# U of batches 2 to 7 as seven block products, with sums of x taken from the P V banks

## The chip, the cores and the metric

The kernel runs on one core of one Trainium2 chip. The metric is the device time of one launch in microseconds (us), lower is better: 511.04 us before the change, the median of 3 runs (510.77 to 511.21). TensorE (PE) multiplies, loads its stationary operand by LDWEIGHTS (PEld) and writes PSUM; VectorE (DVE) and ScalarE (ACT) read PSUM and SBUF; GpSimd (POOL) works on SBUF; every DMA is issued from SyncE's queue (SP), in order.

## The reference

```python
# attention: 8 batches, 8 heads, S = 576, head size 64
scores = scale * np.matmul(q, k.transpose(0, 1, 3, 2))
# heads 0-3: the last 32 positions; heads 4-7: earlier positions of the same residue mod 32
attn = softmax(np.where(masks, scores, -1e9))
x = np.matmul(attn, v)                      # as (B, S, 512)
# feed-forward with a spatial gate, d_ff = 1024
h = np.maximum(x @ w_in, 0.0)
u, v = h[..., :512], h[..., 512:]
v_n = (v - mean(v)) / np.sqrt(var(v) + 1e-6)
v_s = np.einsum('ts,bsd->btd', w_spatial, v_n) + b_spatial[None, :, None]
out = (u * v_s) @ w_out
```

## The kernel before

**Numbers.** A float32 value is kept as a rounded fp32r part and an fp32r remainder, and a product is three matmuls (high x high, high x low, low x high: `PROD`, L69). Splitting a value takes two instructions: `rnd` (L383, on ACT, DVE or POOL) makes the high part, `rest` (L397, on DVE or POOL) subtracts it.

**Attention** runs in 32 units, four per batch: two with local heads (`local_attention`, L471) and two with strided heads (`strided_attention`, L611), two heads each. A unit loads q, k and v, multiplies scores, makes a softmax on DVE and ACT, turns P by a DVE transpose, moves its blocks (`ptl`, `pts`) and multiplies P V into two PSUM banks `po`, from which `evac_x` (L424) writes x: ACT makes the high part, DVE the remainder. q, k, v, `kbd` (the strided k), `pp` and `pl` (P before it is turned) have two buffers each.

**Feed-forward**, per batch: `project_v` (L981, the V stage, 48 matmuls of 512 columns, then relu and normalisation in `chain`, L907), `project_u` (L997, the U stage), `gate` (L1084: the spatial product, then u times it) and `project_out` (L1130, the O stage). U is x @ w_in's left half: 8 tiles (2 halves of the sequence times 4 blocks of 128 features), each 4 x 3 matmuls of 128x288, 96 in all, and ACT writes each tile with relu (L1032). O is written as seven products of 2x2 blocks in place of eight, in a form with 7 multiplications (L1220 to L1258): sums of its operand are made on DVE or POOL (`total`), split into one of two slots `gs[0]`, `gs[1]`, multiplied into PSUM banks that go on accumulating, and combined by `keep` (a copy) and `join` (a DVE addition). All stages share four PSUM banks `m`; `held` keeps two of them out of the round for a time.

**The order** is made by a planner in the kernel (`Program.order`, L185): each operation has a due time (`key`), a cost per engine that may do it, and its dependencies; a list schedule gives each engine's sequence, which is what runs. Numbers in `KEYS` (L40) shift due times. PE runs in that order, so that it waits wherever the next matmul's operand, buffer or bank isn't ready. Batches overlap in pairs: the order of stages is V(b), O(b-1), U(b), gate(b), with one tail product for two batches, V's last 64 rows of both, after the first one's U (`moe_tail`, L1051; it needs x of both).

Of the kernel before, what the change touches and what calls it, by code (L numbers as in the profile page):

```python
# [9 lines left out]
F32 = mybir.dt.float32  # L10
# [30 lines left out]
    "a": (-4467.57, -3072.23, -4097.95, -922.09, -62.58, 1948.86, -54.07, 1313.94,),  # L41
    "v": (-1905.33, 2566.85, -1420.01, -351.81,),
    "u": (2077.2, 2507.69, 3441.61, -704.54,),
    "s": (1600.35, 689.49, 1605.62, -2112.6,),
    "t": (-863.37,),
    "o": (2205.96, 3994.67,),
    "cst": (-3153.23,),
    "wv": (1302.43, 874.44, 1384.1, 1780.19,),
    "wu": (-954.94, -624.77, 1601.45, 150.66,),
    "lead": (10.96,),  # L50
    "fill": (634.17, 3536.74, 3759.85, 2050.78, 1027.03, 2069.52,),
    "dp": (1410.82, -7913.25, 17481.82, 35293.8,),
    "dpt": (1128.82,),
    "lv": (-2407.03, -1707.29, -454.82, -254.06,),
    "lu": (1673.71, 2694.32, 1173.88, 457.25,),
    "lo": (1682.63, -1711.68, 1604.3, -4779.41,),
    "ls": (-1419.42, 1216.18, -2053.61, -239.17, 1173.72,),
    "pre": (2.84, 55.65,),
    "near": (3261.26,),
    "la": (-2830.09, -2292.21, -5019.65, -1683.98, -4639.4, -3037.2, 298.54, 1600.86,),  # L60
    "lb": (-1002.76, 2105.75, -428.93, 3194.59, 1811.71, 608.19, -588.14, 3548.95,),
# [9 lines left out]
U_FIRST = (0,)  # L71
WHOLE = ()
# [59 lines left out]

class Ring:
# [14 lines left out]
class Program:  # L148
# [3 lines left out]
    def __init__(self):  # L152
        self.ops, self.writer, self.readers, self.spare = [], {}, {}, {}
        self.tiled, self.port, self.kind = {}, {}, {}

# [176 lines left out]
def attention_moe(ctx, tc, qT, kT, ks, vl, vs, cst, eye, w_in, w_out, wsp, wtail, out):  # L332
# [11 lines left out]
    cst_sb = sb.tile([P, 3, 2 * STRIDE], F32, name="cst_sb")  # L344
    mask_l0, mask_l, mask_s = cst_sb[:, 0], cst_sb[:, 1], cst_sb[:, 2, :RA]
# [27 lines left out]
    r_bn = Ring(sb, "bn", [P, 12], F32, 3)  # L373
# [7 lines left out]
    held = set()  # L381
# [40 lines left out]
    xs = {}  # L422

    def evac_x(due, whole, x_t, o_ps, w, c0, src, dst, extra=0):  # L424
        if whole:
            evac(due - 1, w, lambda: f32(dst(0)), src, [(o_ps,)], [(x_t, 0, c0)], extra=extra)
            return
# [43 lines left out]
    def local_attention(t, due, q, kl, v, vin, kin):  # L471
        p_sb, st, x_t = p_local[t % 2], st_local[t % 2], xs[t]
# [44 lines left out]
        for u in range(nu):  # L517
# [16 lines left out]
            if not masked:  # L534
                add(
                    due - 12.5, [(DVE, 75 + 1.04 * 2 * STRIDE)], f_m,
                    [(s_ps[u % 2],), ("cst",), ("local0", t % 2)], [(p_sb, u), (st, u)],
                )

            def f_e(eng, f0=f0, u=u, m=m):  # L540
# [9 lines left out]
                [(st, u), *([(s_ps[u % 2],), ("local0", t % 2)] if masked else [])],  # L550
# [3 lines left out]
        if t in APART:  # L554
# [5 lines left out]
                [*pin, ("local0", t % 2)], [(st, u) for u in range(nu)],  # L560
# [13 lines left out]
        for i, n, slot, c0, z in LOCAL_MOVES:  # L574
            for k in range(2):
# [12 lines left out]
                ptok.append(("ptl", i, k, c0))  # L588
        for c0 in (0, 3):
            o_ps = r_po.new()  # L590
            w = 3 * LQ

            def f_v(eng, c0=c0, o_ps=o_ps):
# [13 lines left out]
                due, t in WHOLE, x_t, o_ps, w, c0, lambda o_ps=o_ps, w=w: o_ps()[:, :w],  # L607
                lambda i, c0=c0, w=w: x_t()[:, i, c0 * LQ : c0 * LQ + w],
            )

    def strided_attention(t, due, q, k, v, vin, kin):  # L611
        st, x_t = r_st.new(), xs[t]
        nu, w = 2 * SB, 2 * SB * RA
        pp = pps[t % 2]
        ptok = ("pp", t % 2)
# [4 lines left out]
        view = lambda: pp[:, :, :RA]  # L620
        scores = lambda: s_ps()[:, :w].rearrange("p (u k) -> p u k", k=RA)
        zeros_in = ("pp0", t % 2)
        each = lambda ap: ap[:, :, None].to_broadcast([P, nu, RA])

        def f_s(eng):
            for c in range(SB):
                for i in range(4):
# [6 lines left out]
                        kbd[:, t % 2, :, STRIDE + r : STRIDE + r + RA],  # L634
# [7 lines left out]
        if not masked:  # L642
# [40 lines left out]
            lambda eng: eng.transpose(turned(), pp[:]), [ptok], [(pc,)],  # L683
# [8 lines left out]
        half = RA * STRIDE // 2  # L692
# [613 lines left out]
    def setup_sel(eng):  # L1306
        eng.memset(sel, -0.5)
# [154 lines left out]
```

## Time and profile before

| | |
|---|---|
| median of 3 runs | 511.04 us |
| the profiled execution | 509.85 us |
| its span, first to last instruction | 507.8 us |
| PE, PEld busy | 495.6, 455.2 us |
| DVE, ACT, POOL busy | 344.7, 280.3, 111.7 us |
| mean granted TensorE clock | 0.99 |

Busy time of PE is pipelined: a 128x288 matmul is shown with some 296 ns, though in a dense run one starts every 133 ns. DVE instructions overlap in the same way at their ends. An "idle before" is put down to whatever ended it last.

### The profile page before, as it was taken

How to read it: one execution, taken by the hardware profiler on the slowest of the kernel's cores; microseconds unless marked ns; L12 is line 12 of the kernel's file. 1: busy time of each engine (PE TensorE's matmuls, PEld its weight loads, DVE VectorE, ACT ScalarE, POOL GpSimd, SP SyncE). 2: the span in 40 equal slices, each digit the busy share in tenths (PEclk: the TensorE clock that was granted, in tenths of full speed). 3: DMA queues.
4: the chain of work that ended last, by engine and by line, in shares of the span. 5: the costliest groups of instructions: out<-in, count | busy, mean ns of one | idle time of the engine just before them, and what ended most of it. 6: DMA issues, size and time to landing. Idle time of an engine off the chain costs nothing.

```text
span 507.8 us, 15733 instructions
## 1 busy us (share of the span) xinstructions
PE 495.6 (98%) x6398; PEld 455.2 (90%) x6398; DVE 344.7 (68%) x1069; ACT 280.3 (55%) x871; POOL 111.7 (22%) x229
## 2 busy tenths in 40 slices
PE   7599999999999999999999999999999999999997
PEld 4478898889988999899998999989998899989997
DVE  3988898988678628784488925687288841666055
ACT  5897777577546556373654765355554642235214
POOL 3553426133232013020221211121022200120000
PEclk9699999999999999999999999999999999999999
DMA  8996443422423412204224243024131020002002
GB/s 288 397 359 222 125 139 108 137 93 64 144 92 119 127 50 91 90 25 151 81 92 138 76 132 89 4 90 139 60 99 45 1 94 0 1 2 93 1 1 94
DMA packets 26247, 52.71 MB, mean 104 GB/s; under 512 B 3136, under 2 KB 11584, under 8 KB 26176
## 3 DMA queue, kind: packets, MB, share of 16 engines
q1 hardware_dynamic: 26176, 51.72, 31.0%
q8 instruction: 50, 0.82, 0.7%
q14 instruction: 21, 0.17, 0.1%
HBM read 42.27 MB, written 9.44 MB: 102 GB/s over the span
## 4 chain that ended last, share of the span: by engine, by line
PE 95%; DMA 4%; SPq 0%; issue 0%; ACT 0%
PE m L961 21%; PE m L1018 20%; PE m L1099 20%; PE m L1149 18%; PE po L700 3%; PE po L596 3%; DMA q<-qT 3%; PE s L486 2%; PE s L629 2%; PE m L1111 2%; PE m L1112 2%; DMA kbd<-ks 1%; PE po L1378 0%; SPq L420 0%; PE m L629 0%
## 5 line engine op out<-in xcount | busy, mean ns | idle before, releaser
L1099 PE MATMUL m<-wsp_sb,vn 128*128 128x288 f32 x768 | 112.9, 296 | 0.0
L1099 PEld LDWEIGHTS m<-wsp_sb,vn 128*128 128x128 f32 x768 | 105.5, 189 | 0.9
L1018 PE MATMUL m<-x,w_in_sb 128*128 128x288 f32 x768 | 105.3, 297 | 0.0
L1018 PEld LDWEIGHTS m<-x,w_in_sb 128*128 128x128 f32 x768 | 103.0, 188 | 0.6
L961 PE MATMUL m<-w_in_sb,x 128*128 128x512 f32 (+1 forms) x408 | 99.4, 398 | 0.0
L1149 PE MATMUL m<-g,w_out 128*128 128x288 f32 x672 | 92.9, 296 | 0.0
L1149 PEld LDWEIGHTS m<-g,w_out 128*128 128x128 f32 x672 | 89.9, 188 | 1.3
L961 PEld LDWEIGHTS m<-w_in_sb,x 128*128 128x128 f32 (+1 forms) x408 | 74.1, 185 | 18.3
L393 POOL TENSOR_SCALAR ptl<-pc 32x64 f32<-32x64 f32 (+3 forms) x98 | 38.5, 393 | 105.5 <-DVE pc L567 69.5
L916 DVE BATCH_NORM_STATS2 bn<-vv 128x6 f32<-128x512 f32 (+1 forms) x37 | 25.2, 683 | 47.4 <-ACT vv L911 47.1
L391 ACT CAST g<-u 128x288 fp32r<-128x288 f32 x91 | 39.0, 435 | 29.4 <-DVE u L812 13.1
L543 ACT ACTIVATE pl<-pl,ml 128x64 f32<-128x64 f32 (+1 forms) x140 | 47.0, 337 | 7.9 <-DVE ml L523 7.8
L929 POOL TENSOR_TENSOR bn<-bn,sel 128x1 f32<-128x1 f32 (+1 forms) x37 | 21.5, 582 | 130.0 <-DVE bn L924 125.2
L401 DVE TENSOR_TENSOR g<-u,g 128x288 fp32r<-128x288 f32 x98 | 43.6, 459 | 7.5 <-ACT g L391 5.2
L911 ACT ACTIVATE vv<-m 128x512 f32<-128x512 f32 (+1 forms) x37 | 21.9, 596 | 47.0 <-PE m L961 46.7
L1032 ACT ACTIVATE u<-m 128x288 f32<-128x288 f32 x56 | 22.9, 409 | 41.2 <-PE m L1018 40.5
L1121 DVE TENSOR_TENSOR u<-m,u 128x288 f32<-128x288 f32 x56 | 24.9, 453 | 30.5 <-PE m L1112 29.9
L391 ACT COPY ptl<-pc 32x320 f32<-32x320 f32 (+3 forms) x94 | 33.5, 356 | 13.7 <-DVE pc L567 11.9
L413 ACT CAST x<-po 128x288 fp32r<-128x288 f32 x60 | 22.1, 399 | 22.2 <-PE po L700 10.3
L401 DVE TENSOR_TENSOR x<-po,x 128x288 fp32r<-128x288 f32 x64 | 27.3, 447 | 8.4 <-ACT x L413 7.9
L523 DVE CUSTOM_DVE_ANT_0 pl<-s,cst_sb 128x64 f32<-128x64 f32 (+1 forms) x140 | 22.1, 215 | 14.5 <-PE s L486 14.5
L543 ACT ACTIVATION_READ_ACCUMULATOR pl<-pl,ml 128x1 f32 (+1 forms) x140 | 26.3, 188 | 0.0
(128 smaller groups left out, 632.8 us busy)
## 6 DMA issues: line engine op xcount, KB each, us to landing
q<-qT SPq DMA_DIRECT2D x32, 295.0 KB, 4.3
v_raw<-vs SPq DMA_DIRECT2D x15, 512.0 KB, 3.8
v_raw<-vl SPq DMA_DIRECT2D x16, 384.0 KB, 3.7
k<-kT SPq DMA_DIRECT2D x16, 304.0 KB, 4.5
kbd<-ks SPq DMA_DIRECT2D x32, 144.0 KB, 4.9
outT<-o SPq DMA_DIRECT2D x32, 144.0 KB, 1.9
outT<-u SPq DMA_DIRECT2D x28, 144.0 KB, 1.8
vn<-w_in SPq DMA_DIRECT2D x4, 512.0 KB, 7.5
```

The lines of the kernel that those rows point to most:

```text
L391: eng.copy(dst(), src())
L393: eng.tensor_scalar(dst(), src(), 1.0, 0.0, op0=ALU.mult, op1=ALU.add)
L401: eng.tensor_tensor(dst(), src(), f32(hi()), op=ALU.subtract)
L413: eng.copy(dst(), src())
L543: eng.activation(p_sb()[:m, u, :], src, AF.Exp, bias=st()[:m, u : u + 1], scale=SCALE if masked else -1.0, **total,)
L916: lambda eng: eng.bn_stats(bn()[:m, 0:6], v()[:m]), [(v,)], [(bn,)],
L961: eng.matmul(v_ps()[:m, :], x_at(kt)[:, a, :], w_in_sb[:, w, kt, HF:], start=(n == 0 and i == 0), stop=(n == NT - 1 and i == 2),)
L1018: eng.matmul(u_ps()[:, :HS], w_in_sb[:, w, kt, f * P : (f + 1) * P], xs[NHP * b + kt]()[:, a, r], start=(n == 0 and i == 0), stop=(n == NT ...
L1032: lambda eng, u=u, f=f, u_ps=u_ps: eng.activation(flat(u)[:, f * HS : (f + 1) * HS], u_ps()[:, :HS], AF.Relu),
L1099: eng.matmul(s_ps()[:, :HS], vn()[:, a, kt, fs], wsp_sb[:, w, kt, r], start=(kt == 0 and i == 0), stop=False,)
L1121: lambda eng, ug=ug, s_ps=s_ps: eng.tensor_tensor(ug(), s_ps()[:, :HS], ug(), op=ALU.mult),
L1149: eng.matmul(o_ps()[:, :HS], w_out_t[0]()[:, w, r, BLOCKS[name], j * P : (j + 1) * P], at(a), start=(first and r == 0 and i == 0), stop=(r ...
```

## The change

- For batches 2 to 7 U becomes `project_u_blocks`: the scheme of seven products that O has, so 7 x 2 x 2 x 3 = 84 matmuls of 128x288 in place of 96. Its left operands are blocks of w_in and four sums of them, which `in_weight_sums` makes once (5 DVE or POOL instructions for each of 4 sums x 2 halves, and the rounding); its right operands are blocks of x and four sums of them.
- The sums of x are made from the P V banks while they are there: `local_sums` one copy and one subtraction of 288 columns for a local unit, `strided_sums` six subtractions of 144 columns for a strided one. Then each sum is split into `gs` (2 halves x rnd and rest).
- The sums live in the second buffers of q, k and `kbd`, the sums of the weights in the second buffers of v, `pp` and `pl` and in a new tile. From unit 8 on (batch 2) attention has one buffer of each of these (`only`, `half`).
- U is written by `keep` (8 copies) and `join` (6 additions) without relu; the gating product makes the relu (one instruction in place of one).
- `sel` and `zeros` lose their tiles, the rings `mx` and `bn` go from 3 to 2, and all of `KEYS` has other values (two lines shown).

```diff
-    "wu": (-954.94, -624.77, 1601.45, 150.66,),
+    "wu": (1507.37, -2412.73, 850.89, 747.53,),
...
+    "su": (-798.11,),
...
+U_BLOCKS = tuple(range(2, B))
...
+    alone = NHP * U_BLOCKS[0] if U_BLOCKS else NHP * nb
+    half = lambda t: t % 2 if t < alone else 0
+    only = lambda t: () if t < alone else (1,)
...
-        q, k = r_q.new(), None
+        q, k = r_q.new(only(t)), None
...
-            v = place = r_v.new()
+            v = place = r_v.new(only(t))
...
+            homes = [r_q.new((0,)), r_k.new((0,)), *spare_k]
...
+    def local_sums(b, r, due, o_ps):
...
+        evac(due - 0.8, HS, at(2, r), lambda: o_ps[1]()[:, :HS], [(o_ps[1],)], toks(2, r))
+        add(
+            due - 0.7, [(DVE, 70 + 1.04 * HS)],
+            lambda eng: eng.tensor_tensor(at(0, r)(), at(2, r)(), o_ps[0]()[:, :HS], op=ALU.subtract),
...
+    def strided_sums(b, r, due, views):
...
+        for i, (n, hf, y) in enumerate(((1, 1, 0), (2, 1, 2), (3, 0, 1))):
+            for g, (o_ps, view) in enumerate(views):
...
+                add(
+                    due - 0.7 + 0.1 * i, [(DVE, 70 + 0.52 * HS)],
+                    lambda eng, n=n, y=y, hf=hf, view=view, part=part: eng.tensor_tensor(
+                        part(n), view()[:, RA // 2 * hf : RA // 2 * (hf + 1), :], part(y), op=ALU.subtract
...
+    def in_weight_sums():
+        key = KEYS["su"][0]
+        hv, late = r_v.new((0,)), [r_pp.new((0,)), r_pl.new((0,))]
...
+        for i, (name, a, b, op) in enumerate((
+            ("s1", "21", "22", ALU.add), ("s3", "11", "21", ALU.subtract),
+            ("s2", "s1", "11", ALU.subtract), ("s4", "12", "s2", ALU.subtract),
+        )):
...
+    def project_u_blocks(b, key):
...
+        product(key, "11", direct(0, 0), xb, True)
+        product(key + step, "s1", summed(0, 1), zb, True)
+        for j in range(2):
+            keep(key + step, 0, j, xb[j])
+        product(key + 2 * step, "s2", summed(1, 0), xb, False)
...
+        product(key + 3 * step, "s4", direct(1, 1), zb, False)
...
+        product(key + 4 * step, "s3", summed(2, 1), xb, False)
+        for j in range(2):
+            join(key + 4 * step, 1, j, zb[j])
+        wb = [r_pm.new(held) for _ in range(2)]
+        product(key + 5 * step, "12", direct(1, 0), wb, True)
...
+        product(key + 6 * step, "22", summed(3, 0), xb, False)
...
-                    lambda eng, ug=ug, s_ps=s_ps: eng.tensor_tensor(
-                        ug(), s_ps()[:, :HS], ug(), op=ALU.mult
+                    lambda eng, ug=ug, s_ps=s_ps: (
+                        eng.scalar_tensor_tensor(
+                            ug(), ug(), 0.0, s_ps()[:, :HS], op0=ALU.max, op1=ALU.mult
```

PE in the U stage of batch 2, before: tile after tile, each of the four blocks of x in turn (`x_13` to `x_16`).

```order
L1018 MATMUL m_68_2983<-x_13_1569,w_in_sb_62 128x288 x3
L1018 MATMUL m_68_2983<-x_14_1837,w_in_sb_62 128x288 x3
L1018 MATMUL m_68_2983<-x_15_2036,w_in_sb_62 128x288 x3
L1018 MATMUL m_68_2983<-x_16_2172,w_in_sb_62 128x288 x3
L1018 MATMUL m_69_3015<-x_13_1569,w_in_sb_62 128x288 [waits DVE_49]
```

The same stage after the change (line 1163; `g` holds a split sum of x, `pp_3` and `pl_3` a sum of weights): the products of four blocks stand among each other, and P V of unit 14 (line 721) follows, which waits for its v.

```order
L1163 MATMUL m_66_2919<-g_7_1600,pp_3_1897 128x288 [waits Activation_49,Pool_49]
L1163 MATMUL m_66_2919<-g_7_1600,pp_3_1897 128x288 x2
L1163 MATMUL m_67_2926<-g_7_1600,pp_3_1897 128x288 [waits Activation_49]
L1163 MATMUL m_67_2926<-g_7_1600,pp_3_1897 128x288 x2
L1163 MATMUL m_66_2919<-g_7_1600,pl_3_2220 128x288 [waits Pool_49]
L1163 MATMUL m_66_2919<-g_7_1600,pl_3_2220 128x288 x2
L1163 MATMUL m_67_2926<-g_7_1600,pl_3_2220 128x288 x3
L1163 MATMUL m_72_3093<-x_15_1989,w_in_sb_62 128x288 [waits DVE_49]
L1163 MATMUL m_72_3093<-x_15_1989,w_in_sb_62 128x288 x2
L721 MATMUL po_28_3098<-pts_68,v_raw_20_3055 64x2x18 [waits DMAHW0_49,PE_49]
```

So U waits for sums, their splits and bank copies on three engines; P V of units 13 and 14 now lie inside the stage and those of 15 and 16 right behind it, where before the stage began with units up to 15 done.

SP's queue around the loads of v for units 17 and 18, before; odd and even numbers of `v_raw` are the two buffers, so a load waits for the P V of the last unit but one.

```order
L420 DMA v_raw_16_2916<-vl 128x768 [waits DMAHW5_49,PE_49]
L420 DMA q_18_2988<-qT 128x590 [waits DMAHW6_49,PE_49]
L420 DMA k_10_2998<-kT 128x608 [waits DMAHW7_49]
L420 DMA v_raw_17_3193<-vs 128x1024 [waits DMAHW0_49,PE_49]
L420 DMA q_19_3200<-qT 128x590 [waits DMAHW1_49,PE_49]
L420 DMA k_11_3210<-kT 128x608 [waits DMAHW2_49]
```

The same queue after, from unit 14 of the program (`v_raw_20`) on: only even numbers, one buffer, so each load of v waits for the P V right before it.

```order
L438 DMA v_raw_20_3055<-vs 128x1024 [waits DMAHW0_49,PE_49]
L438 DMA q_28_3065<-qT 128x590 [waits DMAHW1_49,PE_49]
L438 DMA k_16_3071<-kT 128x608 [waits DMAHW2_49]
L438 DMA v_raw_22_3140<-vs 128x1024 [waits DMAHW3_49,DMAHW0_49,PE_49]
L438 DMA v_raw_24_3280<-vl 128x768 [waits DMAHW4_49,DMAHW3_49,PE_49]
L438 DMA q_30_3292<-qT 128x590 [waits DMAHW5_49,DMAHW1_49,PE_49]
```

DVE while PE is in U of batch 2 and takes P V of units 13 and 14, after the change (L419 `rest`, L791 and L806 sums of x, L1194 `join`; before, DVE held here the L401 rows on x, a softmax and nothing of U):

```order
L419 TENSOR_TENSOR g_6_1532<-kbd_67,g_6_1532 128x288 [waits Pool_49]
L457 TENSOR_SCALAR ml0_72<-ml0_72 128x10 [waits Activation_49]
L461 RECIPROCAL ml0_72<-ml0_72 128x10 [waits DVE_49]
L419 TENSOR_TENSOR x_18_3014<-po_27_2996,x_18_3014 128x288 [waits PE_49,Activation_49]
L466 TENSOR_TENSOR pl_0_74<-pl_0_74,ml0_72 128x640 [waits DVE_49]
L791 TENSOR_TENSOR q_17_2994<-kbd_67,po_26_3006 128x288 [waits Activation_49]
L419 TENSOR_TENSOR x_18_3014<-po_26_3006,x_18_3014 128x288
L1194 TENSOR_TENSOR u_5_2966<-m_68_2912,u_5_2966 128x288 [waits DMAHW5_49,DMAHW2_49,DMAHW6_49,DMAHW1_49,PE_49]
L1194 TENSOR_TENSOR u_5_2966<-m_69_2950,u_5_2966 128x288 [waits PE_49]
L1194 TENSOR_TENSOR u_5_2966<-m_66_2919,u_5_2966 128x288 [waits PE_49]
L1194 TENSOR_TENSOR u_5_2966<-m_67_2926,u_5_2966 128x288 [waits PE_49]
L806 TENSOR_TENSOR k_9_3138<-po_28_3098,q_17_2994 128x9x16 [waits Activation_49]
```

DVE gets new work in a stage in which it had little; the sums of a unit come before the bank it reads is free for the next P V.

## Rows read from the trace of the kernel before

**Rows 1.** The page: busy time by engine; the span in 40 slices for PE, DVE and the granted clock.

```profile
PE 495.6 (98%) x6398; PEld 455.2 (90%) x6398; DVE 344.7 (68%) x1069; ACT 280.3 (55%) x871; POOL 111.7 (22%) x229
PE   7599999999999999999999999999999999999997
...
DVE  3988898988678628784488925687288841666055
...
PEclk9699999999999999999999999999999999999999
```

**Rows 2.** All waits of PE: what waited for what, us in total, times, longest.

```profile
PE m L486 <- DMA q<-qT: 6.4, 1, 6.4
PE s L1378 <- DVE zeros L1332: 0.9, 1, 0.9
PE m L629 <- DMA k<-kT: 0.7, 1, 0.7
PE po L700 <- issue: 0.6, 1, 0.6
PE m L629 <- DMA q<-qT: 0.3, 1, 0.3
```

**Rows 3.** The chain that ended last, in order of time (start us, us, what): a whole U stage, a whole V stage, a whole O stage.

```profile
293.90 12.80 PE m L1018 x96
...
388.16 11.20 PE m L961 x48
...
454.63 11.10 PE m L1149 x84
```

**Rows 4.** Busy time by stretch (us; PE, PEld, DVE, ACT, POOL; granted clock; DMA share, GB/s): 60 us early, 10 us of it, a V stage with the beginning of O, and three U stages (in the first DVE makes one local unit of attention: its two remainders of x, ten maxima, the normalisation and the turn).

```profile
60.00:120.00 60.00, 60.00 (x870) 54.55 (x869) 53.50 (x192) 45.90 (x157) 21.17 (x39) 1.00 0.34 108
...
90.00:100.00 10.00, 10.00 (x56) 8.79 (x56) 9.83 (x28) 5.37 (x17) 1.53 (x3) 1.00 0.50 167
...
388.00:413.00 25.00, 25.00 (x264) 22.42 (x263) 22.12 (x59) 14.16 (x36) 5.09 (x10) 1.00 0.16 53
...
172.00:186.00 14.00, 14.00 (x198) 13.71 (x191) 4.41 (x26) 8.55 (x35) 2.23 (x7) 1.00 0.35 106
...
294.00:307.00 13.00, 13.00 (x98) 12.92 (x97) 2.06 (x4) 7.33 (x27) 2.31 (x7) 1.00 0.28 82
...
413.00:426.00 13.00, 13.00 (x98) 12.95 (x97) 0.00 (x0) 3.48 (x9) 0.00 (x0) 1.00 0.10 32
```

**Rows 5.** Groups by line and shape (busy us, mean ns of one, idle before): the additions and splits of 288 columns, an addition of 256, a remainder of 512, a scalar_tensor_tensor from PSUM, a short one, ACT's copy, relu and cast, POOL's cast.

```profile
L401 DVE TENSOR_TENSOR g<-u,g 128x288 fp32r<-128x288 f32 x98 | 43.6, 459 | 7.5 <-ACT g L391 5.2 <-POOL g L393 1.5
L1121 DVE TENSOR_TENSOR u<-m,u 128x288 f32<-128x288 f32 x56 | 24.9, 453 | 30.5 <-PE m L1112 29.9
L401 DVE TENSOR_TENSOR vn<-vv,vn 128x512 fp32r<-128x512 f32 x32 | 21.9, 686 | 3.7 <-ACT vn L391 3.6
L645 DVE SCALAR_TENSOR_TENSOR pp<-s,cst_sb 128x288 f32<-128x288 f32 x14 | 6.2, 446 | 3.0 <-PE s L629 3.0
L812 DVE TENSOR_TENSOR g<-g 128x256 f32<-128x256 f32 x6 | 2.8, 474 | 0.1
L924 DVE TENSOR_SCALAR bn<-bn 128x1 f32<-128x1 f32 x35 | 5.1, 146 | 0.4
L413 ACT COPY u<-m 128x288 f32<-128x288 f32 x28 | 11.1, 399 | 8.9 <-PE m L1149 8.8
L1032 ACT ACTIVATE u<-m 128x288 f32<-128x288 f32 x56 | 22.9, 409 | 41.2 <-PE m L1018 40.5 <-ACT u L1032 0.5
L391 ACT CAST g<-u 128x288 fp32r<-128x288 f32 x91 | 39.0, 435 | 29.4 <-DVE u L812 13.1 <-PE m L1149 8.7 <-DVE u L1121 6.4
L393 POOL TENSOR_SCALAR g<-u 128x288 fp32r<-128x288 f32 x7 | 3.0, 432 | 9.1 <-PE m L1149 6.8 <-ACT w_out L391 2.1
```

**Rows 6.** DVE in order of time (start us, us of the piece, count): a dense run of 288-column instructions; and one of 256 columns beside a POOL cast.

```profile
92.46 0.80 DVE L401 TENSOR_TENSOR g<-u,g 128x288 fp32r<-128x288 f32 x2
...
96.14 0.17 DVE L920 BATCH_NORM_AGGREGATE bn<-bn 128x2 f32<-128x6 f32 x1
...
87.08 0.42 DVE L812 TENSOR_TENSOR g<-g,g 128x256 f32<-128x256 f32 x1
87.23 1.60 POOL L393 TENSOR_SCALAR w_out<-g 128x512 fp32r<-128x512 f32 x2
87.53 0.77 DVE L812 TENSOR_TENSOR g<-g 128x256 f32<-128x256 f32 x1
```

**Rows 7.** In order of time: a P V of a strided unit with the load of v that waits for its end, and the scores of a local unit; then loads of v by their time from issue to landing (two short stretches, and the least, median and most from 120 to 480 us).

```profile
281.07 1.14 PE L700 MATMUL po<-pts,v_raw 64*64 64x36 f32 x64
282.30 0.34 SPq L420 DMA_DIRECT2D v_raw<-vl  x1
...
175.75 0.97 PE L486 MATMUL s<-k,q 64*32 64x64 f32 x72
...
v_raw<-vs SPq DMA_DIRECT2D x1, 512.0 KB, 3.8
...
v_raw<-vs SPq DMA_DIRECT2D x1, 512.0 KB, 4.3
...
DMA to landing us min/median/max: 2.9/3.7/5.2
```

**Rows 8.** PE in order of time: six records (three matmuls) of the warm-up that the planner puts into early gaps.

```profile
30.82 1.48 PE L1378 MATMUL po<-zeros 128*32 128x256 f32 x6
```

More of the change, by code (lines that the diff above doesn't have):

```diff
@@ L559, in local_attention @@
                 ),
-                [*pin, ("local0", t % 2)], [(st, u) for u in range(nu)],
+                [*pin, ("local0", half(t))], [(st, u) for u in range(nu)],
             )
@@ L733, in attention @@
         if local:
-            k = r_k.new()
+            k = r_k.new(only(t))
             load(fetch_k, k, kT[b, hp], [(k,)], P * (STRIDE + S) * 4)
@@ L746, in attention, with block_sums @@
         (local_attention if local else strided_attention)(t, due, q, k, v, [(place,)], kin)
+    def block_sums(b):
+        if b not in sums:
+            for j in range(2):
+                before = spare_k[j].users if spare_k[j] else prog.users([("k", 1, j), ("k0", 1)])
+                spare_k[j] = Place(lambda j=j: kbd[:, 1, j], before)
+            homes = [r_q.new((0,)), r_k.new((0,)), *spare_k]
+            got = lambda n: homes[n].tile() if n > 1 else homes[n]()
+            sums[b] = (
+                lambda n, r: lambda: got(n)[:, r * HS : (r + 1) * HS],
+                lambda n, r: [(homes[n], r, g) for g in range(2)],
+            )
+        return sums[b]
@@ L1036, in project_u, with product, fn, direct @@
                 )
+    in_sums = {}
+    def project_u_blocks(b, key):
+        at, tok = sums.pop(b)
+        u = [r_u.new() for _ in range(2)]
+        us[b, 0], us[b, 1] = u
+        step = 1.5
+        def product(key, name, src, bank, first):
+            w_at, w_tok = in_sums[name]
+            for r in range(2):
+                op, toks = src(r, key + 0.74 * r)
+                for j in range(2):
+                    def fn(eng, r=r, j=j, op=op):
+                        for i, (w, a) in enumerate(PROD):
+                            eng.matmul(
+                                bank[j]()[:, :HS], w_at(w, r)[:, j * P : (j + 1) * P], op(a),
+                                start=(first and r == 0 and i == 0), stop=(r == 1 and i == 2),
+                                skip_group_check=not first,
+                            )
+                    add(
+                        key + 0.74 * r + 0.37 * j, [(PE, 3 * pe_cost(P, HS))], fn,
+                        toks + w_tok[r], [(bank[j],)],
+                    )
+        def direct(k, hf):
+            return lambda r, key: (
+                lambda a: xs[NHP * b + 2 * k + r]()[:, a, hf * HS : hf * HS + HS], x_tok(NHP * b + 2 * k + r),
+            )
+        def summed(n, slot):
+            def src(r, key):
+                g = gs[slot]
+                op = lambda a: g()[:, 2 * r + a]
+                split(key - KEYS["pre"][0], HS, op, (g, r), at(n, r), tok(n, r))
+                return op, [(g, r, 0), (g, r, 1)]
+            return src
+        def keep(key, hf, f, bank):
+            evac(key, HS, block(u[hf], f), lambda: bank()[:, :HS], [(bank,)], [(u[hf], f)])
+        def join(key, hf, f, bank):
+            dst = block(u[hf], f)
+            add(
+                key, [(DVE, 70 + 1.04 * HS)],
+                lambda eng: eng.tensor_tensor(dst(), bank()[:, :HS], dst(), op=ALU.add),
+                [(bank,)], [(u[hf], f)],
+            )
+        xb, zb = ([r_pm.new(held) for _ in range(2)] for _ in range(2))
+        held.update(x.n % 4 for x in xb)
+        product(key, "11", direct(0, 0), xb, True)
+        product(key + step, "s1", summed(0, 1), zb, True)
+        for j in range(2):
+            keep(key + step, 0, j, xb[j])
+        product(key + 2 * step, "s2", summed(1, 0), xb, False)
+        for j in range(2):
+            keep(key + 2 * step, 1, 2 + j, zb[j])
+        product(key + 3 * step, "s4", direct(1, 1), zb, False)
+        for j in range(2):
+            keep(key + 3 * step, 1, j, xb[j])
+        product(key + 4 * step, "s3", summed(2, 1), xb, False)
+        for j in range(2):
+            join(key + 4 * step, 1, j, zb[j])
+        wb = [r_pm.new(held) for _ in range(2)]
+        product(key + 5 * step, "12", direct(1, 0), wb, True)
+        for j in range(2):
+            join(key + 5 * step, 1, 2 + j, xb[j])
+        product(key + 6 * step, "22", summed(3, 0), xb, False)
+        held.clear()
+        for j in range(2):
+            join(key + 6 * step, 0, j, wb[j])
+            keep(key + 7 * step, 0, 2 + j, xb[j])
@@ L1277, in attention_moe @@
     starts, knots, at = [], [(0.0, NHP)], 0.0
+    lasts = lambda kind, b: cost[kind] - 1.5 * (kind == "u" and b in U_BLOCKS)
     for kind, b in plan:
@@ L1283, in attention_moe @@
         starts.append(at)
-        at += cost[kind]
+        at += lasts(kind, b)
     if nb <= lead:
```

196 lines of the change are left out of this document (131 added, 65 removed).

## Prediction

> **What bounds the kernel now.** Read the waits of PE first [rows 2]: 8.9 us in all, every one of them on the input, the set-up or an "issue" at the start; after that PE waits for nothing. The page says the same [rows 1]: PE is at 9 tenths or more from the third slice to the last but one, and the granted clock is near full (2.4 GHz) in every slice but the second, in which PE stood waiting. So the chain that ended last is PE's own list of matmuls, and its stages give the price of one [rows 3]: U 12.80 us for 96, 133.3 ns each; V 11.20 for 48 of 512 columns, 233.3 ns; O 11.10 for 84, 132.1 ns. The 296 ns that the page shows for a matmul is its length, not its price. DVE is the next engine, 344.7 us [rows 1], but unevenly spread: 53.5 of 60 us early, 22.1 of 25 in a V stage, 2.1 and 0.0 of 13 in two U stages [rows 4]. PE did not wait in any of these, not even where DVE was busy for 9.83 of 10 us.
>
> The reader should take two questions from this: how many matmuls go, and whether anything new can come later than PE in a list that has no slack of its own.
>
> **The sum, part by part.** All against the profiled execution: 509.85 us, of which 507.8 are the span and 2.05 lie around it; the median of the runs, 511.04, is 1.19 above it, and I add that at the end.
>
> *Removed on PE.* Six batches x (96 - 84) = 72 matmuls x 133.3 ns = **-9.6 us**, all on the path, since U runs back to back on PE [rows 3]. The new products have the same shape, so the price is the same (132.1 ns by the O stage, which has this very form: -9.5). Nothing else on PE changes, except the warm-up: the order has 14 warm-up matmuls where it had 12, and one costs 1.48/3 = 0.5 us [rows 8]. They stand in early gaps where PE would wait anyway: 0 to +1.0; the order of loads at the start also changes, and q of unit 2, for which PE waited 6.4 us [rows 2], now has some 200 KB less ahead of it in SP's queue, about half a us at the early rate. I take 0 for the start, with -0.7 to +1.0 as bounds.
>
> *Added on DVE, per batch of 2 to 7.* Eight remainders (four sums x two halves), six joins and two sums of a local unit, all of 288 columns, at 43.6/98 = 0.445 us [rows 5]: 7.1 us. Twelve sums of 144 columns from PSUM: no such row stands in the trace; a one-column instruction takes 0.15 and a 288-column one 0.45, so 1.8 to 5.4 us; I take the line through 288 and 512 columns (0.459 and 0.686 us, so 1.0 ns a column), 0.31 each, 3.7. Together 10.8, in six batches 65 us. The sums of the weights add 20 additions and 8 remainders of 256 columns on DVE at 0.474 [rows 5]: 13.3, once. DVE comes to 423 us of some 500, 85%; in a dense run a 288-column instruction follows the last after (96.14 - 92.46)/10 = 0.368 us [rows 6], and by that it is nearer 80%.
> The gating product costs what it did (446 for a scalar_tensor_tensor, 453 for the product) and so does ACT's copy in place of the relu (399, 409) [rows 5]. ACT gets the local copies and most casts of the sums, about 34 x 0.42 = 14 us on 280 [rows 1], and POOL some 40 short casts, 17 us on 112: neither is near its limit.
>
> *Where the added work meets PE.* In the U stage itself DVE has 8 remainders and 6 joins, 5 to 6 us, plus the sums of the units whose P V stand there, about 4 us, in some 14 us with two units' P V and scores: it fits into what was 0 to 4.4 us of work [rows 4]. The O stage runs the same chain of split, product, keep and join, with more of it, and 84 matmuls take 11.10 us with no wait [rows 3]. So I put these chains at 0, with +0.4 us for the place where one of the pairs' tail products waits for the last unit of attention, whose sums and remainders now come one behind the other on DVE (bounds 0 and 1.5: three pairs at one 288-column instruction more, 0.45, each). If a bank is read too late, what queues behind it on PE is the next P V.
>
> *The early third.* Here the cover is thin. Before, DVE did 53.5 us in 60 [rows 4]. The sums of the weights (13.3) and batch 2's sums of x (4.5) make 71.3. The order takes three units of attention out of it (at the start of batch 2's U, P V is done up to unit 12, before up to 15), and a unit's DVE work is 4.4 us (the first U stage of [rows 4]): 58.1, in 58 us or so of PE. Dense, at 0.368 in place of 0.445, it is about 48. Between the two a wait of PE is likely but short. I take +1.2 us; bounds 0 and 5.
>
> *One buffer in place of two.* From unit 8 on a load of v can start only when the last P V is over. SP issues it 0.1 us after that (282.21, 282.30) and it lands after 2.9 to 5.2 us, median 3.7; with q right behind it 3.8 and 4.3 [rows 7]. In the order PE has this much work between two P V of a batch's neighbours: scores 0.97 [rows 7] and 24 matmuls x 0.133, 4.1 us, at the shortest for a strided unit. Twelve places have such short distances: five of 4.0 to 4.1 us, five of 4.5 to 4.8, and two of 3.7 before a local unit, with its smaller load. Against 0.1 + 3.7 + 0.1 none waits, against 4.3 + 0.2 five wait 0.4 (2 us), and if all landed like the slowest, 5.4 in all: 5 x 1.35 + 5 x 0.75 + 2 x 1.7 = 13.9 us. I take +0.5 (nearest to the median). q and k have 8 us and more between two scores, so they are not late.
> The Trainium skill ("Trainium Kernel Development and Optimization", Best Practices) says to double-buffer so that DMA overlaps compute, and this part does the opposite. The trace of before can't show the loss, since its loads had two buffers; that loss is the third rival.
>
> *POOL beside DVE.* A 256-column addition with both inputs in SBUF took 0.77 us where its neighbour took 0.42, while a POOL cast was running [rows 6]; so each added cast of 0.43 on POOL can cost DVE up to 0.35. Forty of them, all met, are 14 us of DVE, most of it where DVE is idle; it is inside the bounds of the early third and gives no term.
> The Trainium skill ("SBUF — State Buffer", Who interferes with whom) calls the port pair of DVE and GpSimd an exclusive lock, held for the whole instruction, which an addition with two SBUF inputs takes too; that row agrees with it. By that rule the sums kept in SBUF cost more than by the plain row of 0.45, at most the same 14 us of DVE.
>
> **Sum:** 509.85 - 9.6 + 0 + 0.4 + 1.2 + 0.5 = 502.35; with 1.19 for the median **503.5 us**.
>
> **The rivals.**
> 1. *DVE becomes the bound* in the early third and in batches 2 to 4. For it: 58 us of work for 58 us of PE, and DVE's waits for other engines don't vanish. Against it: PE did not wait beside 9.83 of 10. Price: the upper bound 5 early plus 0.5 in each of two later pairs, in place of 1.2: 508.3 us at most, 506 to 508.
> 2. *The saving is eaten in the U stage*: four of seven products wait for a split and banks for a keep or join. For it: split is ACT 0.435 and DVE 0.45, 0.9 us and the hand-overs, and now lies ahead of PE in a stage that only had ACT behind it. Against it: the O stage. Price: 0.4 us x 4 products x 6 batches = 9.6, so 511 to 513: no change or a little slower.
> 3. *The single buffer of v*, the other side: at each of the twelve places PE stands until v lands. It decides from the point where these waits pass 511.0 - 503.0 = 8.0 us, 0.67 a place; with 4.24 us of PE work at the mean place and 0.2 for the hand-overs that is when v lands after 4.7 us on the mean, where median and most are 3.7 and 5.2 [rows 7]; at the most, 13.9 us, the time is 503 + 13.4 = 517. For it: one load of v with q behind took 4.3. Against it: nothing else big is on the queues in these stretches (DMA share 0.10 to 0.35 in the V and U stages [rows 4]).
>
> **Chances.** The forecast, 501 to 505.5: 0.68. The first rival, 505.5 to 508.5: 0.14. The second: 0.07, about half of it within 0.2% (1 us, what a measurement of this kernel can tell from no change). The third: 0.07 slower than 512. Better than 501 (a shorter start and no wait at all): 0.04. So faster 0.87, same 0.04, slower 0.09. The range 500.8 to 508.5 leaves out the slower cases and little of the better one, some 15 in 100; the forecast's own range is 501 to 505.5.
>
> **What the profile of after would show.** Right: 84 matmuls in a U stage; PE's busy time down by 8 to 10 us; DVE near 420; PE's waits after the start adding up to 1 to 4 us, some before P V on v, some in the first 130 us on DVE. Rival 1 shows as PE waiting on DVE rows between 90 and 140 us; rival 2 as waits of line 1163 on ACT or DVE in every batch; rival 3 as waits of line 616 or 721 on v, twelve times. A start that ends PE's first wait much later than 17 us, or a granted clock below full after a wait, would make the forecast wrong altogether.

## The result, and the profile after

The changed kernel is slower: 516.35 us as the median of 4 runs (515.21 to 517.83) against 510.9 us of before beside it, a ratio of 1.0112 with a 95% interval of 1.0082 to 1.0141. I had forecast 503.5 us and a gain. The profiled execution, the slowest of the four, took 517.83 us; its span is 515.8 us, 8.0 us more than the span of before. In the first experiment below two of ten runs, the profiled one among them, took 937 us; they are left out of its numbers, and nothing is read from that trace.

The page of after, the lines that answer to [rows 1]:

```profile
PE 492.4 (95%) x6330; PEld 447.1 (87%) x6330; DVE 409.2 (79%) x1268; ACT 288.2 (56%) x899; POOL 132.7 (26%) x269
...
PE   6698999999999999999999989999899999999997
...
DVE  4899989999999878887797947979588775658455
...
PEclk9699999999999999999999989999999999999999
```

PE is busy for 3.2 us less and yet the span is longer, so PE stood. VectorE is at 409, even less than the 423 that I had reckoned. PE's row has slices of 8 at 39, 297 and 361 us, where before had none below 9 between the second slice and the last, and the granted clock has one at 297, too. All waits of PE, as in [rows 2] (what waited for what, us in total, times, longest):

```profile
PE m L504 <- DMA vn<-w_in: 6.0, 1, 6.0
PE m L1163 <- ACT u L431: 4.4, 3, 2.2
PE m L1284 <- DVE u L1194: 1.5, 4, 0.4
PE s L650 <- issue: 1.2, 1, 1.2
PE m L1337 <- DVE u L1360: 1.0, 1, 1.0
...
PE po L721 <- DMA v_raw<-vs: 0.8, 1, 0.8
PE m L1296 <- DVE tail L419: 0.8, 1, 0.8
PE po L616 <- DMA v_raw<-vl: 0.5, 1, 0.5
```

The first is the old wait at the start (6.4 us in [rows 2]). The second is new and the largest: the block products of U (line 1163) wait for ScalarE's copy of a bank into u (line 431, `keep`). The third is the gate's first matmul behind VectorE's `join`, in four of six batches. A wait costs more than its own length: the matmul ahead of it takes the 296 ns that the page shows, where in a dense run the next one starts after 133. So I counted for each piece of PE's list the time from its start to the next start, less its matmuls at the prices of a dense run, as in [rows 3]; this is an estimate. By it before loses 12.4 us, 11.8 of them in the first 60; after loses 28.5, 13.3 of them in the first 60. The work itself became 9.4 us shorter (481.3 to 471.9 us at those prices), which is the saving, and the two added warm-up matmuls are 1.0. 16.1 + 1.0 - 9.4 = 7.7 of the 8.0 us.

What does the copy wait for? U(4), PE first and ScalarE below it (start us, us, what; idle before and its releaser in brackets):

```profile
297.60 1.77 PE L1163 MATMUL m<-g,su_sb 128*128 128x288 f32 x12
301.57 0.66 PE L1163 MATMUL m<-x,w_in_sb 128*128 128x288 f32 x3 [2.20 <-ACT u L431]
302.18 2.19 PE L616 MATMUL po<-ptl,v_raw 128*64 128x96 f32 x24
```

```profile
296.93 0.67 ACT L431 COPY u<-m 128x288 f32<-128x288 f32 x2
...
301.12 0.70 ACT L431 COPY u<-m 128x288 f32<-128x288 f32 x2 [2.85 <-DMA outT<-u]
```

and SyncE's queue in the same stretch:

```profile
292.18 1.81 SPq L438 DMA_DIRECT2D q<-qT  x1
294.11 0.36 SPq L1368 DMA_DIRECT2D outT<-o  x1
294.51 0.43 SPq L438 DMA_DIRECT2D k<-kT  x1
295.35 1.03 SPq L1368 DMA_DIRECT2D outT<-o  x2
296.48 0.98 SPq L1368 DMA_DIRECT2D outT<-u  x2
```

O(3) puts its last two output tiles into u[1], blocks 0 and 1, and stores them from there. The two stores are issued from 296.48 on, behind a load of q and one of k (295 and 304 KB), and the chain of waits has the second of them, for which PE stood, at 4.07 us to landing:

```profile
296.95 4.07 DMA outT<-u
```

U(4) began at 294.43. After its third product PE needs a bank again, and the copy of that bank (`keep(key + 2 * step, 1, 2 + j, zb[j])`) is the first one into u[1]. It goes to block 2, not to the two blocks that are being stored, yet it starts 0.1 us after the second store has landed, at 301.12, and so do those at 241.02 and 365.30. So it seems that the tile is handed over as a whole; a finer hand-over was not tried.

The stores are not later than they were. In before the same two stores of O(3) also stand behind a load of q and one of k, and they took 5.2 us to landing:

```profile
292.90 0.41 SPq L420 DMA_DIRECT2D q<-qT  x1
293.35 0.44 SPq L420 DMA_DIRECT2D k<-kT  x1
293.89 0.38 SPq L1180 DMA_DIRECT2D outT<-o  x1
294.36 0.92 SPq L1180 DMA_DIRECT2D outT<-u  x2
```

```profile
outT<-u SPq DMA_DIRECT2D x2, 144.0 KB, 5.2
```

So they landed 5.7 to 6.1 us behind the beginning of U(4) (293.90 in [rows 3]), against 6.2 to 6.6 us in after. But the U of before wrote the four blocks of u[0] first and came to u[1] at 301.99, 2 us after the landing. What is new is the order in which U fills its tiles.

By U(7) no load of attention is left, and SyncE issues the stores of O(6) one behind the other:

```profile
473.24 3.24 SPq L1368 DMA_DIRECT2D outT<-o  x4
476.52 0.92 SPq L1368 DMA_DIRECT2D outT<-u  x2
```

The last two are issued 1.3 us behind the stage's beginning (in U(4) 2.05), but nothing runs beside them, they land after 1.9 us, and U(7)'s 84 matmuls go through in 11.11 us. This piece of the chain is the counterpart to the U stage of [rows 3]:

```profile
475.21 11.11 PE m L1163 x84
```

A wait of this length has a tail, as the table by stretch shows (PE, PEld, DVE, ACT, POOL busy; granted clock; DMA share, GB/s):

```profile
298.00:301.50 3.50, 1.37 (x11) 1.11 (x9) 1.24 (x3) 0.66 (x4) 1.14 (x3) 1.00 0.34 118
301.50:305.50 4.00, 3.93 (x99) 3.42 (x99) 2.75 (x7) 2.52 (x9) 0.00 (x0) 0.58 0.04 8
```

PE was busy for 1.37 of 3.5 us, and in the next 4 us the granted clock is 0.58, near the lower of its two levels (1.2 of 2.4 GHz): another 1.3 us of PE's list. With it and with what a wait costs beyond its length, the waits at 241, 301 and 365 us cost 6.2 us of PE's time by the count above.

### The profile page after: what moved, and what is told of

Same layout as the page of the kernel before. It is cut to its first block, busy times and chain, and to the rows that moved or that the text cites. A ratio compares the mean times of both kernels' runs of the same rounds, so it can differ in the third digit from the quotient of the medians.

```text
span 515.8 us, 16002 instructions
## 1 busy us (share of the span) xinstructions
PE 492.4 (95%) x6330; PEld 447.1 (87%) x6330; DVE 409.2 (79%) x1268; ACT 288.2 (56%) x899; POOL 132.7 (26%) x269
## 4 chain that ended last, share of the span: by engine, by line
PE 74%; DVE 9%; DMA 7%; ACT 6%; issue 2%; SPq 1%; POOL 0%; ACTq 0%; DVEq 0%
PE m L1284 19%; PE m L1070 17%; PE m L1337 13%; PE m L1163 8%; PE m L1127 5%; PE po L616 3%; PE po L721 3%; DMA outT<-u 2%; PE s L504 2%; ACT pl L561 2%; PE m L1296 2%; PE m L1297 2%; PE s L650 2%; DVE g L419 1%; DMA vn<-w_in 1%
## 5 line engine op out<-in xcount | busy, mean ns | idle before, releaser
L409 ACT CAST g<-u 128x288 fp32r<-128x288 f32 x79 | 33.9, 433 | 38.4 <-DVE u L876 20.7
L411 POOL TENSOR_SCALAR ptl<-pc 32x64 f32<-32x64 f32 (+3 forms) x92 | 36.1, 392 | 55.6 <-DVE pc L585 30.2
L1038 POOL TENSOR_TENSOR bn<-bn,cst_sb 128x1 f32<-128x1 f32 (+1 forms) x37 | 22.1, 601 | 108.4 <-DVE bn L1033 96.2
L419 DVE TENSOR_TENSOR g<-u,g 128x288 fp32r<-128x288 f32 x98 | 43.1, 458 | 5.7 <-ACT g L409 5.0
L409 ACT COPY ptl<-pc 32x320 f32<-32x320 f32 (+3 forms) x100 | 35.9, 359 | 10.6 <-DVE pc L585 8.7
L1163 PE MATMUL m<-x,w_in_sb 128*128 128x288 f32 x216 | 34.6, 301 | 4.4 <-ACT u L431 4.4
L431 ACT COPY u<-m 128x288 f32<-128x288 f32 x76 | 28.1, 402 | 17.4 <-PE m L1163 7.9
L1163 PEld LDWEIGHTS m<-x,w_in_sb 128*128 128x128 f32 x216 | 29.9, 188 | 5.9 <-ACT u L431 5.1
L411 POOL TENSOR_SCALAR pts<-pc 32x288 f32<-32x288 f32 x36 | 17.8, 494 | 56.5 <-PE po L721 40.5
L1045 DVE TENSOR_SCALAR vv<-vv,bn 128x512 f32<-128x512 f32 (+1 forms) x37 | 20.6, 557 | 11.8 <-POOL bn L1038 11.3
L419 DVE TENSOR_TENSOR x<-po,x 128x288 fp32r<-128x288 f32 x64 | 27.2, 447 | 2.9 <-ACT x L431 1.6
L1307 DVE SCALAR_TENSOR_TENSOR u<-u,m 128x288 f32<-128x288 f32 x48 | 21.0, 448 | 10.1 <-PE m L1297 10.1
```

What stands on the lines that cost most here:

```text
L409: eng.copy(dst(), src())
L411: eng.tensor_scalar(dst(), src(), 1.0, 0.0, op0=ALU.mult, op1=ALU.add)
L419: eng.tensor_tensor(dst(), src(), f32(hi()), op=ALU.subtract)
L431: eng.copy(dst(), src())
L1038: lambda eng: eng.tensor_tensor(bn()[:m, 9:10], bn()[:m, 8:9], sel[:m, 0:1], op=ALU.pow),
L1163: eng.matmul(bank[j]()[:, :HS], w_at(w, r)[:, j * P : (j + 1) * P], op(a), start=(first and r == 0 and i == 0), stop=(r == 1 and i == 2), ...
```

## Experiments

Theory 1: the loss is in buffers that are handed over, the stores of u first. Theory 2: VectorE is too full with the sums of x. Theory 3: one buffer for v. Ratios are to the runs of before beside them, with their 95% interval in brackets; after stands at 1.0112.

**Stores from a constant.** In `project_out`, for an O that a block U follows:

```diff
-            store(key + 7 * step, 2 + j, 0, mine(1, j), [(u[1], j)])
+            far = (lambda j=j: f32(wsp_sb[:, 0, j, :HS])) if b + 1 in U_BLOCKS else mine(1, j)
+            store(key + 7 * step, 2 + j, 0, far, [(u[1], j)])
```

> The last two of the eight output stores of each O stage that a block U follows read a constant tile instead of u (those two pieces of the output are not the reference's); everything else, order and bytes of the DMA queue too, stays. Theory 1 (hand-over): U's copies of the banks into u[1] wait for these stores, so ScalarE's wait for outT<-u at 238, 297 and 362 us goes, with the lowered clock behind it: 4.9 us of waits and 1.3 us of clock, 516.4 - 6.2 = 510.2, at least 511.5. Theory 2 (VectorE is too full with the sums of x): no change, 515.5 to 517. Theory 3 (one v buffer, loads that start late): no change either.

Measured: 510.5 us (the median of eight runs), 1.0011 [0.9997, 1.0025], some 5 us less than after, as theory 1 said. The hand-over is a cause.

**No sums of x.** `local_sums` and `strided_sums` emit nothing for b > 2; the planned order is untouched.

> The fourteen instructions of a batch that make the sums of x from the P V banks (two copies, two differences of 288 columns, twelve of 144... columns in the strided pairs) are issued for batch 2 alone; batches 3 to 7 multiply the sums of batch 2, so their U is wrong. Theory 2 (VectorE): most of the 15 us lost after 60 us goes, 506 or less. Theory 1 (hand-over): the wait for the stores stays; only the joins that stood behind sums (2.1 us), some of the waits at the tail and at O (about 1 us) go: 513 to 514.5.

Measured: 511.29 us, 1.0022 [1.0005, 1.0038]. More than theory 1 allowed, less than theory 2 did. The waits for the gate's join are gone, and the copies into u wait 2.6 us in place of 4.4. The rows of after show how a sum costs PE. VectorE at the end of U(3) (line 806 the sums, 1194 the join, 419 a remainder of x):

```profile
249.19 0.52 DVE L806 TENSOR_TENSOR k<-po,q 128x144 f32<-128x144 f32 x2 [1.54 <-ACT x L431]
249.63 0.30 DVE L806 TENSOR_TENSOR kbd<-po,kbd 128x144 f32<-128x144 f32 x1
250.18 0.31 DVE L806 TENSOR_TENSOR kbd<-po,kbd 128x144 f32<-128x144 f32 x1 [0.25 <-ACT x L431]
250.40 0.81 DVE L419 TENSOR_TENSOR x<-po,x 128x288 fp32r<-128x288 f32 x2
251.13 0.51 DVE L806 TENSOR_TENSOR kbd<-po,k 128x144 f32<-128x144 f32 x2
251.56 0.81 DVE L1194 TENSOR_TENSOR u<-m,u 128x288 f32<-128x288 f32 x2
```

The unit's six sums stand ahead of the join on VectorE, and the gate's first matmul, at 252.07, waits for the join. Here it is not VectorE's share that counts but what stands in front of one instruction.

**Stores issued by ScalarE** (the same output): the last two u stores of an O through `nc.scalar.dma_start`.

> Same output as the reference's: the last two u stores of each O are issued by ScalarE, right behind its own copies, not by SyncE behind the loads of q and k. Theory 1: they start as soon as the copy is done and land about 2 us later (median of outT<-u is 1.9 us), before U's third copy wants the block about 5 us after U begins; ScalarE's wait shrinks from 4.9 us to under 1 us and the time comes to 510.5 to 512. Theory 2 and 3: 515.5 to 517.

Measured: 512.61 us, 1.006 [1.0039, 1.008], a little above theory 1's range. PE's wait for the copies is 0.7 us now, but the stores still take long to land; the rows of u's stores from 60 to 480 us (KB each, median us from issue to landing):

```profile
outT<-u SPq DMA_DIRECT2D x14, 144.0 KB, 1.8
outT<-u ACTq DMA_DIRECT2D x10, 144.0 KB, 3.7
```

Those at O(3)'s end are issued at 294.12 and 294.73 (in after from 296.48 on) and run beside the same loads; what was gained is the earlier issue. The Trainium skill ("DMA: Bandwidth & Descriptors", Issuing engines are not separate DMA queues) says that DMAs of all issuing engines run on the same 16 DMA engines, and a second issuer saves only the time of issuing; the 3.7 us agrees with it, hardly less than the 4.07 of after.

**Seven products in U(6) and U(7) alone**: `U_BLOCKS = (6, 7)`.

> U as seven products in batches 6 and 7 alone (U_BLOCKS = (6, 7)), the relu in the gating product there alone, attention double-buffered until batch 6; the planner orders anew with the keys of after. Theory 1: U(6) and U(7) ran in after without the wait for a store, so the saving of 24 x 133.3 ns = 3.2 us stays, against a start that cost up to 2.5 us more: 508 to 510.5. Theory 2: in the tail of the kernel VectorE is empty and early it has its old load: 507 to 508. Theory 3: 508 to 510.5 with waits for v only behind unit 24.

Measured: 521.68 us, 1.0231 [1.0204, 1.0258], against all three theories. One wait, in O(5), is most of it; of VectorE two of its rows there, the first one of the sums of the weights, which from 351.75 to 358.9 us fill VectorE but for two rows:

```profile
359.45 1.78 PE L1337 MATMUL m<-g,w_out 128*128 128x288 f32 x6 [8.11 <-DVE u L1360]
```

```profile
357.85 0.41 DVE L876 TENSOR_TENSOR vv<-vv 128x256 f32<-128x256 f32 x1
...
358.86 0.45 DVE L1360 TENSOR_TENSOR u<-m,u 128x288 f32<-128x288 f32 x1
```

The sums of the weights have the key -798, so they precede everything else as soon as their buffers are free, here in the middle of O(5). In after they run from 107 to 135 us. Three of these additions stand shortly ahead of the row of line 1360 for which PE waits 1.0 us at 127.9, in the list above; in the run with the old U and the same keys, below, that wait is not there.

**Stores on ScalarE and no sums**, then also **short loads of v** (one block of 12 or 16 from unit 12 on):

> Stores on ScalarE as in the run before this one, and the sums of x issued for batch 2 alone (batches 3 to 7 multiply batch 2's sums, so their U is wrong). If the wait for the stores and the load on VectorE are two causes that add up, the ratio falls by both savings, less the 1.7 us by which the run without sums had already shortened the wait for the stores: after stood at 1.0112, the stores took 0.0052, the sums 0.0090 off it: about 0.997 to 1.000 (1.0112 - 0.0142 + 0.003), 508.5 to 510. If one cause shows itself twice (VectorE late, so the stores late), the two do not add: 1.002 as without the sums alone.

Measured: 510.15 us, 1.0012 [1.0001, 1.0023]: between the two answers. The sums give 0.5% here and gave 0.9% alone; the waits for the copies have come back in part, 1.9 us in this trace where the stores on ScalarE alone had 0.7.

> The same, and from unit 12 on the load of v brings one of its 12 or 16 blocks (each issue still waits for the P V before it; P V multiplies the v of unit 11, so the outputs are wrong). Theory 3 (one v buffer): the waits of P V for v, 1.2 us in the run with the stores on ScalarE, go and the time falls by 1 to 2 us against the run without sums. If more comes back (3 us or over), the loads of v also held up what stands behind them in SyncE's queue.

Measured: 509.14 us, 0.9983 [0.9968, 0.9998]. By the ratios the long loads of v into one buffer are worth 1.5 us, by the medians 1.0: a tenth of what I had allowed at most. That it is P V's waiting is not shown: without the short loads P V waits for v only 0.2 us in the trace, and short loads also leave the DMA engines less to move.

**The old U with the new keys**: `U_BLOCKS = ()`.

> U_BLOCKS = (): every U as before, no sums, two buffers everywhere, the relu in ScalarE's copy; what is left of the change is its table of keys with the tiles that were merged. Theory: the start with the new keys lost 13.3 us of PE instead of 11.8 and ran two more warm-up matmuls (1.0 us); no store is waited for and no v: 512 to 513 (1.003 to 1.006). If the keys suit the old U badly elsewhere: over 513; if the start costs nothing: 510.

Measured: 512.1 us, 1.0041 [1.0028, 1.0054]: the start costs 2.1 us, for behind 46 us PE waits for nothing in this trace. It has the pause that after has at 43 us (1.2 us, "issue") and as many warm-up matmuls.

**Other banks next**: `r_pm.n += 2` after `held.clear()` in U and in O, on top of the stores on ScalarE.

> Same output as the reference's: stores on ScalarE, and after U's and O's last products the next stage takes the two m banks that were joined a step earlier, not the two that the last product has just filled (the planner orders anew). Theory: the gate's first matmul no longer waits 0.35 us for the last copy or join, 4 to 6 times 0.5 us lost, nor U's first for O's: -2 to -3 us against the stores on ScalarE alone: ratio 1.000 to 1.003. If those waits are VectorE's queue behind the sums and not the bank, they stay: 1.005 to 1.007.

Measured: 514.93 us, 1.0101 [1.0076, 1.0126]. A miss: the planner's order changes with the banks, and copies that stood right before are now late (PE waits 2.5 us for them in U and 2.0 at the gate).

**All three causes out at once**: constant source, no sums, short loads of v, in the order of after.

> All three suspected causes taken out of after at once, its order kept: the last two u stores of each O read a constant tile, the sums of x are issued for batch 2 alone, and the loads of v bring one block from unit 12 on (outputs wrong in all of that). If these three are the whole loss behind 60 us, what is left is the saving of 72 matmuls (9.6 us), the start (2.1 us by the run with the old U) and some 2 to 3 us at O(0) and the tails: 510 - 9.6 + 2.1 + 2 = 504 to 505.5, ratio 0.988 to 0.991. If the saving itself is not there, or a fourth cause stands behind, 508 or more (0.997 and above).

Measured: 505.45 us, 0.9916 [0.9899, 0.9933], at the upper end of what was expected. After the first 60 us PE's waits are these and two of 0.2 us (line 1355 is O's product there, 1314 the tail's):

```profile
PE m L1355 <- DVE u L1378: 1.0, 1, 1.0
PE m L1314 <- DVE tail L419: 0.8, 1, 0.8
```

So the saving is there, and the three causes together are what took it. Of the 9.6 us 4.3 show here; the start (2.1) and these waits (2.2) make up 4.3 of the 5.3 that are missing, and the last 1.0 is not taken apart. From 1.0112 over 1.006, 1.0012 and 0.9983 to 0.9916 the steps are 0.52, 0.48, 0.29 and 0.67%, in all 10 us, 5 to 6 of them the stores.

**O's last tiles in the vv ring** (the same output, as in all that follow):

```diff
-            keep(key + 7 * step, mine(1, j), xb[j], [(u[1], j)])
-            store(key + 7 * step, 2 + j, 0, mine(1, j), [(u[1], j)])
+            o = r_vv.new()
+            keep(key + 7 * step, lambda o=o: o()[:, :HS], xb[j], [(o,)])
+            store(key + 7 * step, 2 + j, 0, lambda o=o: o()[:, :HS], [(o,)])
```

with other keys and planner's costs, three times:

> Same output as the reference's. O's last two tiles are copied to the vv ring's two tiles, which nothing uses until the next tail or V stage, not to u, so U never waits for their stores; the planner is given slower DMA landings and 2% slower ScalarE, VectorE and GpSimd work, and the table of keys is searched anew for that. Theory 1: no wait of ScalarE for outT is left in U, the order has slack for late loads: 505 to 509 (0.990 to 0.998). Rival: one buffer each for q, k, kbd and v with the sums on VectorE costs more than 9.6 us whatever the order: 510 to 514.

Measured: 520.57 us, 1.021 [1.0192, 1.0228]. No wait for a store is left, but with the slower costs assumed the order has other waits: 2.2 us of an O for VectorE, 1.7 at the tails, 2.0, 1.9 and 1.6 at the start.

> The same code as the run before it with the planner's own costs and a table of keys searched for those. The order is as tight as after's: without the stores' wait, with joins and loads that come late by tenths of a us: 508 to 512 (0.996 to 1.004). If the tight order was not what cost the time, it lies with or below the run with the slower costs.

Measured: 515.32 us, 1.0117 [1.0095, 1.0139], above the 508 to 512 of a tight order and below the run with the slower costs, so the tightness is not what cost the time; an O now waits 2.4 us for VectorE. Taking the stores out of the way is not enough while all six batches are in blocks.

> Same output as the reference's: seven products in U(6) and U(7) alone, O's last tiles in vv, keys searched from those of before, so the start is planned as in before. Saving 24 x 133.3 ns = 3.2 us, two buffers for all units but the last eight: theory 1 says 506.5 to 508.5 (0.993 to 0.997); rival (single buffers cost what two blocks save): 509.5 to 511.

Measured: 509.13 us, 0.9986 [0.9972, 0.9999], between the two answers and a little below before. With the same code and keys, four, five and six batches in blocks:

> The kernel with U(6) and U(7) in blocks (ratio 0.9986), same code and keys, with U(4) to U(7) in blocks: 24 matmuls fewer, 3.2 us. Price per batch (about 1.5 us of joins, copies and late v, as the stores on ScalarE showed): nothing more is gained, 508.5 to 510 (0.997 to 1.000). Price of the early batches: 506 to 507 (0.992 to 0.994).

Measured: 506.91 us, **0.992 [0.9893, 0.9947]**, as the price of the early batches had it.

> Same, U(3) to U(7) in blocks: another 12 matmuls, 1.6 us. Price per batch: as with four, 0.997 to 1.001. Price of the early batches: still a little less than with four if batch 3 is late enough, else the turn shows here.

Measured: 507.52 us, 0.9941 [0.9919, 0.9964]: no faster than with four; the intervals overlap.

> Same, U(2) to U(7) in blocks as in the change, with the start planned as in before and O's last tiles in vv. Price per batch: 0.998 to 1.002. Price of the early batches: a step up against five batches by over 2 us, with waits of PE between 90 and 190 us.

Measured: 514.15 us, 1.0054 [1.003, 1.0078]. The step is between five and six batches, 5.8 us by the ratios, and most of it is in one place, at 141 us (1.9 us more in an O, at 175). The run with six batches: its longest wait after the start, two stretches (columns as above), and VectorE at the end of the wait:

```profile
PE m L1284 <- DVE x L1310: 3.8, 1, 3.8
```

```profile
137.40:141.10 3.70, 0.01 (x1) 0.00 (x0) 3.70 (x12) 1.14 (x3) 0.00 (x0) 0.81 0.00 0
141.10:147.20 6.10, 6.04 (x27) 6.04 (x28) 5.96 (x33) 3.04 (x10) 1.93 (x5) 0.56 0.01 4
```

```profile
139.99 0.41 DVE L419 TENSOR_TENSOR w_in_sb<-vv,w_in_sb 128x256 fp32r<-128x256 f32 x1
140.33 0.41 DVE L876 TENSOR_TENSOR vv<-vv 128x256 f32<-128x256 f32 x1
140.66 0.81 DVE L1310 TENSOR_TENSOR x<-m,x 128x288 f32<-128x288 f32 x2
```

The sums of the weights fill VectorE while the gating product (line 1310) of batch 1, which frees a bank for PE, stands behind them; PE does nothing for 3.7 us and then runs at 0.56 of its clock for about 6. With four batches they fall from 238 to 249 us, where PE waits for nothing.

> Five batches in blocks with the keys of late stages searched anew: 1 to 2 us below the run with five batches and the keys of two, if the order is what makes joins and v late; the same time within 1 us, if it is not.

Measured: 506.21 us, **0.9905 [0.9881, 0.9929]**, 1.3 us below five batches with the old keys: the order is part of the price. This run and those with four and five batches and the old keys beat both kernels. The page of the run with four, and two of its waits:

```profile
PE 488.4 (97%) x6350; PEld 447.5 (88%) x6350; DVE 391.1 (77%) x1210; ACT 293.2 (58%) x906; POOL 118.3 (23%) x244
```

```profile
PE po L721 <- DMA v_raw<-vs: 1.0, 2, 0.7
...
PE m L1284 <- DVE u L1194: 0.4, 1, 0.4
```

## Why the prediction was wrong

- *72 matmuls x 133.3 ns, -9.6*: right. The work at these prices fell by 9.4 us, U(7) ran in 11.11 us, and with the three causes taken out the time fell below before.
- *"The O stage runs the same chain ... So I put these chains at 0"*: this is the step that failed. The chain's own price is indeed near nothing, as U(7) shows, and the 0.4 us waits on each of four products that the second rival feared did not come: line 1163 waits for ScalarE in three of six batches, each time for stores. But U runs right behind an O that is still storing from the tile into which U's third copy goes, and O has no such stage before it. I read the O stage for the speed of the chain and did not ask who still reads its destination. In place of 0 stand 4.4 us of waits and 1.8 of what they cost beyond their length, the lower clock included; the gate's join behind the sums of x is another 1.5 us of waits, some 2.1 by the count above.
- *The tails, +0.4*: waits of 0.8, 0.3 and 0.2 us. The longest is not the sums': it stands in the run with all three causes out, too, where no sums are made for that pair. There are 27 matmuls of the gate between the pair's last product and its use, where before had 42; that this is the reason is argued, not tried.
- *"q and k have 8 us and more between two scores, so they are not late"*: true for the scores, beside the point for SyncE's queue. In the trace the loads of q and k stand ahead of the stores, but they did so in before, with two buffers, as well.
- *The start, 0*: +2.1 us by the old U with the new keys, above my bound of +1.0.
- *The early third, +1.2*: 1.0 us in after, at 127.9; that the size fits is luck in part, since VectorE was not too full. (The sums of the weights are 24 additions, not 20, at 0.42 us in place of 0.474, so that the 13.3 us stand.) From 60 to 120 us PE had no wait, with VectorE busy for 56.33 of 60 us, as this row against the first of [rows 4] says:

```profile
60.00:120.00 60.00, 60.00 (x807) 55.04 (x806) 56.33 (x193) 42.09 (x136) 23.05 (x43) 1.00 0.27 88
```

  The mechanism of the first rival is nevertheless the one that decides between five and six batches in the last runs: not a full VectorE, but a closed block of its work ahead of one instruction.
- *One v buffer, +0.5*: 1.3 us of waits in after's rows, 1.0 to 1.5 by experiment. The third rival named the right sign and the wrong buffer; its 503 + 13.4 = 517 should start from 503.5.
- *What would make it wrong*: "a granted clock below full after a wait" is what the trace shows at 301.5 us. And PE's waits from 60 us on add up to 9.9 us, where 1 to 4 were forecast after the start.

## What to carry to other kernels

When a stage gets a chain that another stage already runs without a wait, look up for each destination who read it last and when that read is over: an output store counts until it has landed, not until it is issued. These stores landed as late before the change, and nothing showed it, because the tile was needed later; a new order of writing is enough to bring such a wait to light. And work done once, like the sums of the weights, needs a place where nothing stands behind it: the run with four batches, where they fall from 238 us on, is 7 us faster than the one with six, though 24 more matmuls stay in it.

## What I had not expected

- Waits of a few us in the middle of the kernel were followed by some us at a lower granted clock: after 1.37 busy us in 3.5 it was 0.58 for 4 us; after 3.7 idle us 0.56 for 6 (the run with six batches and vv); in O(5) of the run with U(6) and U(7) alone 0.55 for 5.3 us behind a wait of 8.1.
- Two runs with one order of PE's list up to there differ at the "issue" pause at 43 us: 1.2 us in after, with full clock behind it, 2.05 us with the short loads of v, where the next 3 us have a clock of 0.50:

```profile
45.00:48.00 3.00, 3.00 (x11) 2.35 (x9) 3.00 (x6) 0.70 (x1) 1.84 (x3) 0.50 0.54 155
```

What the pause waits for, the traces do not show.
